# Two bf16 reciprocals moved as one 32-bit word, and the softmax scale carried by the state

## The chip, the cores and the metric

The kernel runs on one core of a Trainium2 chip. Its metric is the device time of one execution in microseconds, as the median of several runs; lower is better. The core has a matrix engine (TensorE; PE in the profile, with PEld for its weight loads), a vector engine (DVE), an activation engine (ACT), a general engine (POOL) and a queue engine (SP) that issues most of the transfers.

## The reference

Two stages: an attention in both directions between the tokens x and a small state, for 8 batches of 8 heads, 512 tokens, 32 state rows and 64 features; then a two-layer network with a leaky rectifier over the result.

```python
scale = 1.0 / np.sqrt(D)                                   # D = 64, so 1/8
scores = scale * np.matmul(x, state.transpose(0, 1, 3, 2))
a = softmax over the 32 state rows (max subtracted, sum + 1e-9)
xread = np.matmul(a, state)
scores2 = scale * np.matmul(state, x.transpose(0, 1, 3, 2))
a2 = softmax over the 512 tokens (the same form)
sread = np.matmul(a2, x)
attn = np.concatenate([xread, sread], axis=2)
x = attn.transpose(0, 2, 1, 3).reshape(B * S, H * D)       # 4352 rows of 512
h = x @ w_in                                               # 512 -> 2048
out = np.maximum(0.01 * h, h) @ w_out                      # 2048 -> 512
```

The two softmax lines are shortened here. Inputs and output are fp32; the products run on bf16 operands.

## The kernel before

**What is multiplied.** The kernel never forms xread. For each batch it forms M = state times w_in, head by head (`a_m`, L376), a matrix of 256 rows (8 heads of 32 state rows, in two groups of 128) by 2048 columns. The first layer is then M transposed times aT, where aT holds the probabilities of the first softmax (`ff1`, L397). ACT applies the leaky rectifier to each product and writes hT in bf16 (L403; L415 for pairs; L967 for the quads of batch 0; L571 for batch 7). The second layer (L608 for batch 0, L679 for the others) uses a form with seven products in place of eight, for which DVE forms sums of parts of hT (`su`, L668) and of w_out (`tw`, L645). The rows of the state (sread) go through the network at the end on their own (`FastIn`, rectifier at L492); that part uses x and w_in alone and not the state tiles.

**The state.** It comes in three pieces. Batches 0 and 1 are loaded first (st0f), cast to bf16 by DVE (stb0, L772) and transposed by PE (`state01`, L160). Batches 2 and 3, and then 4 to 7, are loaded by SP (stf), cast by POOL (stb, L186) and transposed by a DMA that SP issues (st_t, L187). Both the scores (`a_scores`, L216) and M (L376) take their weights from these tiles.

**The first softmax, for batches 1 to 7**, lies over a [128, 1024] tile `sc` of scores: the partitions are 4 groups (two heads each, one of each half of the row) of 32 state rows, the columns are tokens. The maximum over 32 partitions comes from a reduce of DVE that transposes 32x32 blocks (L226); the result has one column for each block of 32 tokens. A broadcast transpose (L234) spreads it again over the 32 rows, DVE subtracts (L239), ACT takes the exponential (L246). The sum goes the same way: a transposing reduce (L251), a small epsilon (L255), a reciprocal in bf16 (L258), a broadcast transpose that spreads it (qb, L263) and the product aT = e1 * qb (L264).

**The second softmax** lies along the columns of the same scores: a maximum with a minus sign (mcol, L288), its scaling (mcols, L290), and the exponential on ACT with this as its bias and the scale as its factor (L296).

**Batch 0** is done apart, at the start, with PE spreading the maxima and reciprocals (L826) and its own exponential (`exp0`, L850).

**The order.** Every engine's instructions run in the order of the source text; nothing is reordered. The loop over batches b = 2 to 7 interleaves, in 16 steps s, the first layer of batch b, the second layer of batch b - 1, and the attention of batch b + 1. The numbers PACE say how many units of the second layer follow each step. `a_probs` stands at s = 7 for most batches, so aT of the next batch is made half a turn before it is used; for batches 1 and 2 it stands ahead of the loop, close before its use. `state_t(0)` (L186 and L187 for batches 2 and 3) is issued between two sums of POOL and its casts of x; `state_t(1)` at b = 2, s = 4.

```python
    weights_sum(1, 0, 4, nc.gpsimd)
    state_t(0)
    ...
    for h in range(NK, H):
        cast_x(2, h, h + 1, POO)
    a_open(a2, 2)
    a_xt_dma(a2)
    ...
    a_probs(a1)
    ...
    pm = a_m(a2, 0, "sc")
    ff(0)
```

At the very start PE runs idle matmuls (`spin`, L142), seven before the transposition of the state and three behind it.

Of the kernel before, what the change touches and what calls it, by code (L numbers as in the profile page):

```python
# [9 lines left out]
P = 128  # L10
B, H, S, D = 8, 8, 512, 64
NS = 32
# [5 lines left out]
SCALE = 1.0 / (D ** 0.5)  # L18
# [4 lines left out]
BF16 = mybir.dt.bfloat16  # L23
FP32 = mybir.dt.float32
AF = mybir.ActivationFunctionType
ALU = mybir.AluOpType
AX = mybir.AxisListType
# [3 lines left out]
def kernel(  # L31
# [9 lines left out]
    nc = tc.nc  # L41
# [4 lines left out]
    att = ctx.enter_context(tc.tile_pool(name="att", bufs=2))  # L46
# [10 lines left out]
    VEC, SCA, POO = nc.vector.tensor_copy, nc.scalar.copy, nc.gpsimd.tensor_copy  # L57
# [4 lines left out]
    st0f = consts.tile([P, 4, D], FP32, name="st0f", tag="st0f")  # L62
# [91 lines left out]
    stb0 = consts.tile([P, 4, D], BF16, name="stb0")  # L154
# [18 lines left out]
    stf = [consts.tile([P, hi - lo, P], FP32, name=f"stf{lo}", tag=f"stf{lo}") for lo, hi in groups]  # L173
    stb = [consts.tile([P, hi - lo, P], BF16, name=f"stb{lo}") for lo, hi in groups]
# [8 lines left out]
                )  # L183

    def state_t(i):
        POO(stb[i][:], stf[i][:])  # L186
        nc.sync.dma_start_transpose(st_t[i][:], stb[i][:].rearrange("p b q -> p (b q)"))  # L187


# [4 lines left out]
    def a_open(a, b):  # L194
        a.b = b
        a.xb = xs[b]
        a.xT = att.tile([P, NT, NK, P], BF16, name="xT", tag="xT")
# [45 lines left out]

    def block_exp(sh, n):
        e1 = att.tile([P, n * NS], BF16, name="e1", tag="e1", bufs=1)
        nc.scalar.activation(out=e1[:], in_=sh[:], func=AF.Exp, scale=SCALE)  # L246
        return e1

    def block_recip(e1, n):
        r1 = att.tile([P, n], FP32, name="r1", tag="r1")  # L250
        nc.vector.tensor_reduce(  # L251
            out=r1[:], in_=e1[:].rearrange("p (c j) -> p c j", j=NS),
            axis=AX.X, op=ALU.add, apply_transpose=True,
        )
        nc.vector.tensor_scalar(out=r1[:], in0=r1[:], scalar1=1e-9, scalar2=None, op0=ALU.add)  # L255
        q1h = att.tile([P, n], BF16, name="qh", tag="qh")
        with nc.allow_low_precision(reason="one rounding, of the finished reciprocal"):
            nc.vector.reciprocal(q1h[:], r1[:])  # L258
        return q1h

    def block_probs(dst, e1, q1h, n):
        q1b = att.tile([P, n, NS], BF16, name="qb", tag="qb", bufs=1)
        nc.vector.transpose(q1b[:], q1h[:, :, None].to_broadcast([P, n, NS]))  # L263
        nc.vector.tensor_tensor(  # L264
            out=dst, in0=e1[:].rearrange("p (g s) -> p g s", g=2),
            in1=q1b[:].rearrange("p (g c) j -> p g (c j)", g=2), op=ALU.mult,
        )

    def a_shift(a, part=None):
# [14 lines left out]
            block_probs(a.aT[:], a.e1, a.q1h, NB)  # L284

    def a_max2(a):
        m2 = att.tile([P, 2], FP32, name="mcol", tag="mcol")
        nc.vector.tensor_reduce(out=m2[:], in_=a.sc[:], axis=AX.X, op=ALU.max, negate=True)  # L288
        a.m2s = att.tile([P, 2], FP32, name="mcols", tag="mcols")
        nc.vector.tensor_scalar(out=a.m2s[:], in0=m2[:], scalar1=SCALE, scalar2=None, op0=ALU.mult)  # L290

    def a_exp2(a, g):
        if g == 0:
            a.e2 = att.tile([P, 2, S], BF16, name="e2", tag="e2", bufs=3)
            a.r2 = att.tile([P, 2], FP32, name="r2", tag="r2", bufs=3)
        nc.scalar.activation(  # L296
            out=a.e2[:, g], in_=a.sc[:, g, :], func=AF.Exp,
            bias=a.m2s[:, g:g + 1], scale=SCALE, accum_out=a.r2[:, g:g + 1],
        )

    def a_probs2(a):
# [92 lines left out]
    def ff1(a, hT, j, later=False):  # L394
        ph = psum.tile([P, S], FP32, name="ph", tag="ph")
        for g in range(2):
            nc.tensor.matmul(  # L397
                ph[:], lhsT=a.M[:, g, P * j:P * (j + 1)],
                rhs=a.aT[:, g, :],
                start=(g == 0), stop=(g == 1),  # L400
            )
        def relu():
            nc.scalar.activation(out=hT[:, j, :], in_=ph[:], func=AF.Prelu, alpha=0.01)  # L403
        return relu if later else relu()

    def ff1_pair(a, hT, j, tag):
        ph = psum.tile([P, 2, S], FP32, name="phw", tag=tag, bufs=1)
        for v in range(2):
            for g in range(2):
                nc.tensor.matmul(  # L410
                    ph[:, v], lhsT=a.M[:, g, P * (j + v):P * (j + v + 1)], rhs=a.aT[:, g, :],
                    start=(g == 0), stop=(g == 1),
                )
        def relu():
            nc.scalar.activation(out=hT[:, j:j + 2, :], in_=ph[:], func=AF.Prelu, alpha=0.01)  # L415
        return relu


    class FastIn:


        R = NK
# [89 lines left out]
    class FastLast:  # L512


        R, Q = 2, S // 2
# [27 lines left out]
        def product(self):  # L543
            r, n = self.todo.pop(0)
            R, Q = self.R, self.Q
            if n == 1:
                self.bank = {
                    k: psum.tile([P, R, Q], FP32, name="pl", tag="ph")[:] for k in (1, 2)
                }
                homes = (("mrowb", 1), ("xT", 2)) if r == 0 else (("e2", 3), ("e2", 3), ("xT", 2))  # L550
                ts = [
                    att.tile([P, (2, 1)[t == "e2"], R * Q], FP32, name="ls", tag=t, bufs=c) for t, c in homes
                ]
                self.sv = dict(zip((1, 6, 5, 7), [t[:, i] for t in ts for i in range(t.shape[1])]))
            bank, sv = self.bank[2 if n in (2, 5, 3) else 1], self.sv
            lhs = {1: self.W[1, 1], 2: self.W[1, 2], 4: self.W[2, 2]}.get(n)
            if lhs is None:
                lhs = self.S[{3: 3, 5: 0, 6: 1, 7: 2}[n]]
            rhs = {1: self.X[1, 1], 2: self.X[2, 1], 3: self.X[2, 2]}.get(n)
            if rhs is None:  # L560
                rhs = self.T[{4: 3, 5: 0, 6: 1, 7: 2}[n]]
            for q in range(R):
                j = R * r + q
                nc.tensor.matmul(  # L564
                    bank[:, q, :], lhsT=lhs[:, P * j:P * (j + 1)], rhs=rhs,
                    start=(n in (1, 2, 5) and q == 0), stop=True, skip_group_check=True,
                )
            flat = bank.rearrange("p q t -> p (q t)")

            def relu(i, c, src):  # L570
                nc.scalar.activation(  # L571
                    out=self.hT[:, 8 * i + R * r:8 * i + R * (r + 1), Q * c:Q * (c + 1)],
                    in_=src.rearrange("p (q t) -> p q t", q=R), func=AF.Prelu, alpha=0.01,
                )

            if n in (1, 6, 7):
                SCA(sv[n], flat)
                self.flush()
            elif n == 5:
                VEC(sv[n], flat)  # L580
            if n in (2, 3):
                k = {2: 1, 3: 6}[n]
                nc.vector.tensor_tensor(out=sv[k], in0=flat, in1=sv[k], op=ALU.add)
                self.late.append((relu, 0, n - 2, sv[k]))
            elif n == 7:
                nc.gpsimd.tensor_tensor(out=sv[5], in0=sv[7], in1=sv[5], op=ALU.add)
            elif n == 4:
                relu(1, 0, flat)
                self.flush()
                self.late.append((relu, 1, 1, sv[5]))  # L590
# [178 lines left out]

    open_xb(0)  # L770
    a_open(a0, 0)
    VEC(stb0[:], st0f[:])  # L772
    spin(7, "py")
    state01()
    spin(3, "py")
# [31 lines left out]
    scn, e10, r0, qb0, m0 = {}, {}, {}, {}, {}  # L807
# [39 lines left out]

    def exp0(u):
        e10[u] = att.tile([P, 2, HT], BF16, name="e0", tag="e0")
        nc.scalar.activation(out=e10[u][:], in_=scn[u][:], func=AF.Exp, scale=SCALE)  # L850

    def eps0(u):
        r0[u] = psum.tile([P, NG], FP32, name="r0", tag="py")
# [73 lines left out]
    q = recip0(0)  # L927
# [7 lines left out]
    q = recip0(1)  # L935
# [6 lines left out]
    class Quad:  # L942
# [21 lines left out]
        def relu(self):  # L964
            n = NK // len(self.tiles)
            for i, t in enumerate(self.tiles):
                nc.scalar.activation(  # L967
                    out=h0[:, self.j + n * i:self.j + n * (i + 1), HT * self.u:HT * (self.u + 1)],
                    in_=t, func=AF.Prelu, alpha=0.01,
                )  # L970

    def m0_evict(c, pm):
# [149 lines left out]
    for b in range(2, B):  # L1122
        hT = hpool.tile([P, 16, S], BF16, name="hT", tag="hT")
        a = att_of[b]
# [14 lines left out]
        for s in range(16):  # L1139
            fast = nxt is None and 4 <= s < 12  # L1140
            if fast:
                n = 1 if s in (7, 11) else 2
# [127 lines left out]
    u, v = [psum.tile([P, 1, HC], FP32, name="yu", tag="ph")[:] for _ in range(2)]  # L1270
# [8 lines left out]
    for n in (1, 2, 6, 5, 7, 3, 4):  # L1279
# [7 lines left out]
        elif n == 7:  # L1287
            nc.gpsimd.tensor_tensor(
                out=ysb[1][:, :, HC:], in0=fs.sv[7][:], in1=fs.sv[5][:], op=ALU.add
# [46 lines left out]
```

## Time and profile before

| what | value |
|---|---|
| runs, median of 3 | 202.02 us (201.66 to 202.12) |
| profiled execution, span from first to last instruction | 199.8 us |
| the profiled execution's own time | its page gives the span alone |
| granted TensorE clock | 1.00 |
| transfers | 28.01 MB, 140 GB/s on average |

A row of the groups is read thus: line, engine, operation, output tile and input tiles, shape of output and input, count, then busy time in us, mean ns of one instruction, and the engine's idle time just ahead of these instructions with what ended it. A row of the timeline has the start in us from the span's start, the length in us, and the instructions merged in it. PE's matmuls overlap in their pipeline, so one matmul of 512 columns is listed with some 380 ns while a row of them advances faster.

### The profile page before, as it was taken

How to read it: one execution, taken by the hardware profiler on the slowest of the kernel's cores; microseconds unless marked ns; L12 is line 12 of the kernel's file. 1: busy time of each engine (PE TensorE's matmuls, PEld its weight loads, DVE VectorE, ACT ScalarE, POOL GpSimd, SP SyncE). 2: the span in 40 equal slices, each digit the busy share in tenths (PEclk: the TensorE clock that was granted, in tenths of full speed). 3: DMA queues.
4: the chain of work that ended last, by engine and by line, in shares of the span. 5: the costliest groups of instructions: out<-in, count | busy, mean ns of one | idle time of the engine just before them, and what ended most of it. 6: DMA issues, size and time to landing. Idle time of an engine off the chain costs nothing.

```text
span 199.8 us, 4974 instructions
## 1 busy us (share of the span) xinstructions
PE 193.2 (97%) x2044; PEld 134.3 (67%) x2066; DVE 160.8 (80%) x249; ACT 143.5 (72%) x263; POOL 55.4 (28%) x82
## 2 busy tenths in 40 slices
PE   7999999999999999999999999999999999999993
PEld 2566633446676767766776677667767788799882
DVE  2676689999999989966997499879978977995622
ACT  3478748599877867877797859787878768767710
POOL 8483174690027004200320041100020024005250
PEclk9999999999999999999999999999999999999999
DMA  5999997999581993269414945290025102210035
GB/s 195 221 206 271 236 296 137 221 286 202 112 223 28 302 266 73 47 213 272 91 24 195 241 43 107 105 164 0 0 108 157 30 0 94 119 56 0 0 95 171
DMA packets 39510, 28.01 MB, mean 140 GB/s; under 512 B 25344, under 2 KB 36736, under 8 KB 39488
## 3 DMA queue, kind: packets, MB, share of 16 engines
q1 hardware_dynamic: 33712, 20.35, 40.8%
q0 software_dynamic: 4944, 6.55, 16.0%
q10 hardware_dynamic: 832, 0.79, 1.2%
q8 instruction: 16, 0.26, 0.5%
q14 instruction: 6, 0.05, 0.1%
HBM read 17.30 MB, written 8.91 MB: 131 GB/s over the span
## 4 chain that ended last, share of the span: by engine, by line
PE 96%; DVE 1%; issue 1%; ACT 1%
PE yq L679 44%; PE ph L397 20%; PE pm L376 4%; PE py L608 4%; PE pyw L608 4%; PE pf L475 3%; PE yu L679 3%; PE ph L958 3%; PE pspin L142 2%; PE pl L564 2%; PE sc L216 1%; PE psn L342 1%; PE php L958 1%; PE phw L410 1%; PE scn L826 1%
## 5 line engine op out<-in xcount | busy, mean ns | idle before, releaser
L403 ACT ACTIVATE hT<-ph 128x512 bf16<-128x512 f32 x100 | 58.5, 605 | 18.4 <-PE ph L397 11.9
L679 PEld LDWEIGHTS <-su 128*128 128x128 bf16 x480 | 45.9, 98 | 14.8 <-DVE su L668 0.8
L397 PE MATMUL ph<-aT,M 128*128 128x512 bf16 x180 | 54.4, 379 | 0.3
L679 PEld LDWEIGHTS <-hT 128*128 128x128 bf16 x336 | 32.3, 98 | 14.3 <-issue 2.5
L679 PE MATMUL yq<-tw_xf,su 128*128 128x256 bf16 x224 | 31.6, 273 | 0.3
L679 PE MATMUL yq<-w_out_bf,hT 128*128 128x256 bf16 x224 | 31.0, 273 | 0.1
L113 POOL CAST xb<-xl 128x512 bf16<-128x512 f32 (+1 forms) x24 | 13.9, 621 | 49.9 <-DMA xl<-in_x_dram 36.7
L668 DVE TENSOR_TENSOR su<-hT 128x1024 bf16<-128x1024 bf16 (+1 forms) x27 | 19.3, 718 | 6.7 <-ACT hT L403 6.7
L397 PEld LDWEIGHTS <-M 128*128 128x128 bf16 x200 | 19.5, 98 | 5.7 <-DVE aT L264 0.2
L751 POOL TENSOR_TENSOR yo<-sv,sv 128x512 f32<-128x512 f32 x7 | 9.1, 1295 | 39.2 <-ACT sv L688 19.4
L688 ACT COPY sv<-yq 128x512 f32<-128x512 f32 x28 | 16.3, 586 | 3.0 <-PE yq L679 2.5
L679 PE MATMUL yq<-w_out_bf,su 128*128 128x256 bf16 x112 | 15.3, 273 | 0.3
L679 PE MATMUL yq<-tw_x,su 128*128 128x256 bf16 x112 | 15.5, 273 | 0.0
L691 DVE TENSOR_TENSOR yo<-yq,sv 128x512 f32<-128x512 f32 x20 | 13.6, 681 | 1.5 <-PE yq L679 1.5
L679 PE MATMUL yq<-tw_x,hT 128*128 128x256 bf16 x104 | 14.5, 273 | 0.0
L390 ACT CAST M<-pm 128x1024 bf16<-128x1024 f32 x12 | 12.2, 1018 | 0.2 <-PE pm L376 0.2
L296 ACT ACTIVATE e<-sc,mcols 128x512 bf16<-128x512 f32 x16 | 11.0, 695 | 0.6 <-DVE mcols L290 0.6
L608 PEld LDWEIGHTS <-hT 128*128 128x128 bf16 x64 | 5.9, 98 | 7.0 <-issue 1.1
L668 DVE TENSOR_TENSOR su<-su,hT 128x1024 bf16<-128x1024 bf16 x14 | 9.7, 692 | 0.5
L288 DVE TENSOR_REDUCE mcol<-sc 128x2 f32<-128x1024 f32 x8 | 9.7, 1214 | 0.0
L226 DVE TRANSPOSE_TENSOR_REDUCE mrow<-sc 128x32 f32<-128x1024 f32 x7 | 8.7, 1240 | 0.5 <-PE sc L216 0.5
L668 DVE TENSOR_TENSOR su<-hT,su 128x2048 bf16<-128x2048 bf16 (+1 forms) x8 | 9.1, 1132 | 0.0
(173 smaller groups left out, 302.6 us busy)
## 6 DMA issues: line engine op xcount, KB each, us to landing
out_dram<-yo SPq DMA_DIRECT2D x12, 512.0 KB, 2.7
xl<-in_x_dram SPq DMA_DIRECT2D x5, 1024.0 KB, 6.7
w_in_bf<-in_moe_w_in_dram POOLq DMA_DIRECT2D x4, 512.0 KB, 7.8
w_out_bf<-in_moe_w_out_dram POOLq DMA_DIRECT2D x2, 512.0 KB, 12.9
x<-in_x_dram POOLq DMA_DIRECT2D x2, 512.0 KB, 11.5
w_out_bf<-in_moe_w_out_dram POOLq DMA_DIRECT2D x4, 256.0 KB, 13.7
xl<-in_x_dram POOLq DMA_DIRECT2D x1, 1024.0 KB, 16.4
out_dram<-ysb SPq DMA_DIRECT2D x4, 256.0 KB, 5.6
```

Source lines behind the costliest of these rows:

```text
L113: copy(xs[b][:, :, h0:h1].rearrange("p t h d -> p h t d"), xl[b][:, h0:h1].rearrange("p h (t d) -> p h t d", t=NT),)
L288: nc.vector.tensor_reduce(out=m2[:], in_=a.sc[:], axis=AX.X, op=ALU.max, negate=True)
L296: nc.scalar.activation(out=a.e2[:, g], in_=a.sc[:, g, :], func=AF.Exp, bias=a.m2s[:, g:g + 1], scale=SCALE, accum_out=a.r2[:, g:g + 1],)
L390: copy(a.M[:, :, cols], pm[:])
L397: nc.tensor.matmul(ph[:], lhsT=a.M[:, g, P * j:P * (j + 1)], rhs=a.aT[:, g, :], start=(g == 0), stop=(g == 1),)
L403: nc.scalar.activation(out=hT[:, j, :], in_=ph[:], func=AF.Prelu, alpha=0.01)
L608: nc.tensor.matmul(y.py, lhsT=hT[:, j, P * i:P * (i + 1)], rhs=w_out_bf[:, j, :], start=(j == 0), stop=(j == 15),)
L668: (eng or nc.vector).tensor_tensor(out=S[n][:, ms], in0=u[:, ms], in1=v[:, ms], op=op)
L679: nc.tensor.matmul(bank[:, i, :], lhsT=lhs[:, m, P * i:P * (i + 1)], rhs=rhs[:, m, :], start=(first and m == 0 and (i == 0 or of is not No ...
L688: copy(t[:], bank)
L691: nc.vector.tensor_tensor(out=dst, in0=bank, in1=self.sv[n][:], op=ALU.add)
L751: nc.gpsimd.tensor_tensor(out=self.yo(1)[:, :, HC:], in0=f.sv[7][:], in1=f.sv[5][:], op=ALU.add)
```

## The change

There are two parts.

The scale 1/8 is put into the bf16 state tiles as they are made: the two casts (L186 on POOL, L772 on DVE) become multiplications by the constant. The scores come out scaled, so the exponentials (L246, L296, L850) lose their factor, and the scaling of the column maxima (L290) is dropped. M comes out scaled as well, so the rectifiers of the token rows (L403, L415, L571, L967) take a factor of 8 ahead of the rectifier. The factor is a power of two.

The reciprocals of the first softmax are spread two at a time. The transposing reduce (L251) now views the columns as blocks of 64 tokens and steps over them by twos, so that the sums of the tokens 2j and 2j + 1 lie side by side. Their bf16 reciprocals form one 32-bit word, and the broadcast transpose (L263) moves 512 such words for each partition rather than 1024 bf16 values. The product (L264) reads the result again as bf16.

```diff
 state_t
-        POO(stb[i][:], stf[i][:])
+        nc.gpsimd.tensor_scalar(out=stb[i][:], in0=stf[i][:], scalar1=SCALE, scalar2=None, op0=ALU.mult)
 block_exp
-        nc.scalar.activation(out=e1[:], in_=sh[:], func=AF.Exp, scale=SCALE)
+        nc.scalar.activation(out=e1[:], in_=sh[:], func=AF.Exp)
 block_recip
-            out=r1[:], in_=e1[:].rearrange("p (c j) -> p c j", j=NS),
+            out=r1[:], in_=e1[:].rearrange("p (c j i) -> p c i j", j=NS, i=2),
 block_probs
-        q1b = att.tile([P, n, NS], BF16, name="qb", tag="qb", bufs=1)
-        nc.vector.transpose(q1b[:], q1h[:, :, None].to_broadcast([P, n, NS]))
+        q1b = att.tile([P, n // 2, NS], FP32, name="qb", tag="qb", bufs=1)
+        pairs = q1h[:].bitcast(FP32)
+        nc.vector.transpose(q1b[:], pairs[:, :, None].to_broadcast([P, n // 2, NS]))
...
-            in1=q1b[:].rearrange("p (g c) j -> p g (c j)", g=2), op=ALU.mult,
+            in1=q1b[:].rearrange("p c j -> p (c j)").bitcast(BF16).rearrange("p (g s) -> p g s", g=2), op=ALU.mult,
 a_max2
-        m2 = att.tile([P, 2], FP32, name="mcol", tag="mcol")
-        nc.vector.tensor_reduce(out=m2[:], in_=a.sc[:], axis=AX.X, op=ALU.max, negate=True)
-        a.m2s = att.tile([P, 2], FP32, name="mcols", tag="mcols")
-        nc.vector.tensor_scalar(out=a.m2s[:], in0=m2[:], scalar1=SCALE, scalar2=None, op0=ALU.mult)
+        a.m2 = att.tile([P, 2], FP32, name="mcol", tag="mcol")
+        nc.vector.tensor_reduce(out=a.m2[:], in_=a.sc[:], axis=AX.X, op=ALU.max, negate=True)
 a_exp2
-            bias=a.m2s[:, g:g + 1], scale=SCALE, accum_out=a.r2[:, g:g + 1],
+            bias=a.m2[:, g:g + 1], accum_out=a.r2[:, g:g + 1],
 ff1 (and in the same way ff1_pair, FastLast and Quad)
-            nc.scalar.activation(out=hT[:, j, :], in_=ph[:], func=AF.Prelu, alpha=0.01)
+            nc.scalar.activation(out=hT[:, j, :], in_=ph[:], func=AF.Prelu, scale=1.0 / SCALE, alpha=0.01)
 the start
-    VEC(stb0[:], st0f[:])
+    nc.vector.tensor_scalar(out=stb0[:], in0=st0f[:], scalar1=SCALE, scalar2=None, op0=ALU.mult)
 exp0
-        nc.scalar.activation(out=e10[u][:], in_=scn[u][:], func=AF.Exp, scale=SCALE)
+        nc.scalar.activation(out=e10[u][:], in_=scn[u][:], func=AF.Exp)
```

More of the change, by code (lines that the diff above doesn't have):

```diff
@@ L414, in relu @@
         def relu():
-            nc.scalar.activation(out=hT[:, j:j + 2, :], in_=ph[:], func=AF.Prelu, alpha=0.01)
+            nc.scalar.activation(out=hT[:, j:j + 2, :], in_=ph[:], func=AF.Prelu, scale=1.0 / SCALE, alpha=0.01)
         return relu
@@ L572, in relu @@
                     out=self.hT[:, 8 * i + R * r:8 * i + R * (r + 1), Q * c:Q * (c + 1)],
-                    in_=src.rearrange("p (q t) -> p q t", q=R), func=AF.Prelu, alpha=0.01,
+                    in_=src.rearrange("p (q t) -> p q t", q=R), func=AF.Prelu, scale=1.0 / SCALE, alpha=0.01,
                 )
@@ L968, in relu @@
                     out=h0[:, self.j + n * i:self.j + n * (i + 1), HT * self.u:HT * (self.u + 1)],
-                    in_=t, func=AF.Prelu, alpha=0.01,
+                    in_=t, func=AF.Prelu, scale=1.0 / SCALE, alpha=0.01,
                 )
```

## The prediction

> **What bounds the kernel now.** I read the page's busy shares and the chain that ended last first, then the busy time by stretches, then what the weight loads of TensorE (PEld) waited for (us in total, times, longest), and only then the single rows of the operations that are edited.
>
> ```profile
> PE 193.2 (97%) x2044; PEld 134.3 (67%) x2066; DVE 160.8 (80%) x249; ACT 143.5 (72%) x263; POOL 55.4 (28%) x82
> ...
> PE 96%; DVE 1%; issue 1%; ACT 1%
> ```
>
> The chain runs through PE for 96% of the span of 199.8 us. DVE, from which nearly everything is taken here, is busy 80% of the time and holds 1% of the chain. An average can hide a stage in which DVE ends last, so the stretches come next.
>
> ```profile
> core 0: us, PE busy (x) PEld busy (x) DVE busy (x) ACT busy (x) POOL busy (x), PEclk, DMA share, GB/s
> ...
> 10.00:17.00 7.00, 6.69 (x137) 4.53 (x130) 5.04 (x11) 5.62 (x11) 5.15 (x7) 1.00 1.24 206
> 17.00:36.00 19.00, 18.84 (x157) 9.43 (x160) 15.22 (x22) 12.68 (x25) 7.43 (x9) 1.00 1.05 237
> 36.00:60.00 24.00, 23.74 (x210) 14.25 (x213) 23.59 (x31) 20.18 (x35) 10.02 (x10) 1.00 0.89 208
> 60.00:100.00 40.00, 39.69 (x415) 27.97 (x420) 35.41 (x53) 30.98 (x57) 9.40 (x13) 1.00 0.63 162
> 100.00:140.00 40.00, 39.68 (x414) 27.81 (x418) 33.39 (x47) 31.59 (x59) 5.28 (x6) 1.00 0.49 109
> 140.00:160.00 20.00, 19.84 (x231) 14.11 (x233) 17.96 (x34) 15.95 (x30) 1.26 (x1) 1.00 0.25 74
> 160.00:185.00 25.00, 24.95 (x286) 22.10 (x286) 20.25 (x30) 18.44 (x35) 6.32 (x5) 1.00 0.14 54
> ```
>
> Between 17 and 185 us PE is idle for 0.16 + 0.26 + 0.31 + 0.32 + 0.16 + 0.05 = 1.26 us in all, at a granted clock of 1.00. That is the ceiling on what any relief of another engine can bring there. Note 36 to 60 us: DVE is busy for 23.59 of 24.00 us and PE still for 23.74. DVE is full there, but just keeps up. What it keeps up with is seen in the waits of the weight loads:
>
> ```profile
> PEld L216 <- DMA xT<-xb: 0.8, 2, 0.4
> PEld L160 <- DVE stb L772: 0.8, 1, 0.8
> PEld L679 <- DVE su L668: 0.8, 2, 0.4
> ```
>
> A load runs beside the previous matmul, so a wait of a load is a bound on a wait of PE, not the wait itself. DVE's sums (su) come in just as they are wanted, twice; the cast of the state (stb) ends a wait once, at the start.
>
> **The change part by part.** First the DVE edits in the attention of batches 1 to 7, by the groups of instructions kept apart by shape (busy us, mean ns of one, idle time before).
>
> ```profile
> L234 DVE STREAM_TRANSPOSE mrowb<-mrow 128x1024 f32<-128x1024 f32 x7 | 8.7, 1245 | 0.2
> L263 DVE STREAM_TRANSPOSE qb<-qh 128x1024 bf16<-128x1024 bf16 x7 | 8.7, 1243 | 0.2
> ...
> L251 DVE TRANSPOSE_TENSOR_REDUCE r<-e 128x32 f32<-128x1024 bf16 x7 | 8.6, 1234 | 0.0
> L239 DVE TENSOR_TENSOR sh<-sc,mrowb 128x1024 f32<-128x1024 f32 x7 | 8.6, 1223 | 0.2
> ...
> L691 DVE TENSOR_TENSOR yo<-yq,sv 128x512 f32<-128x512 f32 x20 | 13.6, 681 | 1.5 <-PE yq L679 1.5
> ...
> L290 DVE TENSOR_SCALAR mcols<-mcol 128x2 f32<-128x2 f32 x8 | 2.0, 245 | 0.3
> ```
>
> The spreading transpose (L263) goes from 1024 16-bit elements to 512 32-bit ones. L234 does the same broadcast transpose on 1024 fp32 elements in 1245 ns against 1243 ns for bf16, so the price goes by elements, not by bytes. For the slope I take the two fp32 rows of one operation: (1223 - 681) / 512 = 1.06 ns per element. A transpose of 512 is then 1243 - 542 = about 700 ns, an estimate, and seven of them free 7 x 0.54 = 3.8 us of DVE. The bounds are 622 ns (half) and 1243 ns (no gain). The multiply behind it (L264) reads the same bytes in the same order and stays.
>
> The reduce (L251) now steps over every second bf16: 1024 elements as before, 4 bytes apart. No row shows a bf16 operand read with a gap. L234 and L239 read fp32 words 4 bytes apart at 1.2 ns per element, and L251 reads dense bf16 at the same 1.2, so packing buys it nothing now and I take 0 for the stride. The bounds are 0 and another 1.23 us each (every element paid twice). [...]
>
> The scaling of the column maxima (L290) goes: 8 x 245 ns = 2.0 us of DVE. Together DVE falls from 160.8 to about 155.0 us. Little of this can reach PE. It is hidden wherever PE runs without a gap, and that is everywhere but the 1.26 us above; were DVE the bound in batches 1 and 2, it would be worth 2 x (0.54 + 0.25) = 1.6 us. The nearest place is the first attention, of batch 1, in the timeline (start us, length us):
>
> ```profile
> 30.00 1.06 ACT L246 ACTIVATE e<-sh 128x1024 bf16<-128x1024 f32 x1 [0.37 <-DVE sh L239]
> ...
> 30.91 1.26 SPq L187 DMA_TRANSPOSE st_t<-stb  x1
> ...
> 31.13 0.17 DVE L290 TENSOR_SCALAR mcols<-mcol 128x2 f32<-128x2 f32 x1
> 31.21 1.24 DVE L251 TRANSPOSE_TENSOR_REDUCE r<-e 128x32 f32<-128x1024 bf16 x1
> ...
> 31.89 1.44 POOL L113 CAST xb<-xl 128x256 bf16<-128x256 f32 x4 [1.00 <-DMA xl<-in_x_dram]
> ...
> 34.37 0.69 DVE L264 TENSOR_TENSOR aT<-e,qb 128x1024 bf16<-128x1024 bf16 x1
> ...
> 35.02 0.11 PEld L376 LDWEIGHTS <-st_t 64*32 64x32 bf16 x8 [0.42 <-DMA st_t<-stb]
> ...
> 35.36 0.55 PEld L397 LDWEIGHTS <-M 128*128 128x128 bf16 x4 [0.23 <-DVE aT L264]
> ```
>
> The probabilities aT are done at 34.37 + 0.69 = 35.06 and the first weight load that waits for them starts at 35.36, behind PE's own product at 35.02. After the change aT comes at about 35.06 - 0.54 - 0.08 = 34.4 (dropping L290 moves the reduce by 0.08 only, from 31.21 to 31.13, since the exponential ends at 31.06). What is late next is PE itself, still in its matmuls. Gain 0 to 0.2 us; I take 0.
>
> Next the scale on ACT. The exponentials lose a constant scale, 124 rectifiers (L403, L415, L571, L967) gain one.
>
> ```profile
> L403 ACT ACTIVATE hT<-ph 128x512 bf16<-128x512 f32 x100 | 58.5, 605 | 18.4 <-PE ph L397 11.9
> ...
> L850 ACT ACTIVATE e<-scn 128x512 bf16<-128x512 f32 x2 | 1.2, 597 | 1.9 <-PE scn L826 1.9
> ```
>
> L850 is an activation of a PSUM tile of this size with a constant scale, L403 one without: 597 and 605 ns. The scale costs nothing that these rows show, and ACT idles 18.4 us ahead of L403 alone. Price 0, within 124 x 8 ns = 1 us either way on an engine with 56 us free.
>
> The start: the state of batches 0 and 1 is now multiplied on DVE (L772) rather than cast.
>
> ```profile
> L772 DVE CAST stb<-st0f 128x256 bf16<-128x256 f32 x1 | 0.5, 546 | 2.4 <-DMA st0f<-in_state_dram 2.4
> ...
> L120 DVE CAST xb<-xf 128x256 bf16<-128x256 f32 x5 | 1.2, 298 | 0.8 <-DMA xf<-in_x_dram 0.8
> ```
>
> And its surroundings in the timeline:
>
> ```profile
> 1.20 3.17 PE L142 MATMUL pspin<-idle 128*128 128x512 bf16 x7 [1.20 <-DVE warm L76]
> ...
> 4.30 0.34 PEld L160 LDWEIGHTS <-stb 128*64 128x64 bf16 x8 [0.84 <-DVE stb L772]
> ```
>
> This one is on PE's path: the load at 4.30 starts when stb is there, and the seventh idle matmul ends at 1.20 + 3.17 = 4.37 by the model, so there is neither cover nor much to gain. The same shape takes 298 ns at L120 and took 546 here. A multiply at one element per 1.06 ns is 681 - 256 x 1.06 = 410 ns, or 658 ns with the 248 ns that L772 took above L120. So -0.1 to +0.1 us; I take 0, since the multiply meets the same neighbours as the cast.
>
> Last, POOL's cast of the later states (L186) becomes a multiply. POOL has no row of a multiply by a constant.
>
> ```profile
> L751 POOL TENSOR_TENSOR yo<-sv,sv 128x512 f32<-128x512 f32 x7 | 9.1, 1295 | 39.2 <-ACT sv L688 19.4 <-issue 18.9 <-POOL ls L586 0.9
> ...
> L186 POOL CAST stb<-stf 128x512 bf16<-128x512 f32 x1 | 1.1, 1067 | 0.0
> ...
> L186 POOL CAST stb<-stf 128x256 bf16<-128x256 f32 x1 | 0.4, 396 | 0.0
> ```
>
> The first, for batches 2 and 3, ends at 30.9, and SP issues its transpose at 30.91. Behind it on POOL stand the casts of x for batch 2, which wait another 1.00 us for their load anyway. The transpose lands here:
>
> ```profile
> st_t<-stb SPq DMA_TRANSPOSE x1, 3.7
> ```
>
> So st_t is there at 34.6 and PE loads it at 35.02: 0.4 us of cover, and from a POOL time of 0.40 + 0.42 = about 0.8 us on, PE waits. Bounds: 0.40 us (the cast) to 1.30 us (a two-input sum of twice the elements), which is 0 to +0.5 us. I take 0.5 us for the multiply, near the cast, as one input is read, and 0 for the time. The second one feeds scores just ahead of this piece of the chain:
>
> ```profile
> L187 SPq DMA_TRANSPOSE st_t<-stb x2: 1189/1226/1262, 30.9 to 62.4; - x2
> ...
> 72.08 0.63 PE psn L342 x64
> ```
>
> Its transpose is issued at 62.4, some 9 us ahead; even a doubled 1.07 us is covered. [...]
>
> Sum against the profiled span: 199.8 + 0 (DVE) + 0 (ACT) + 0 (start) + 0 (POOL) = 199.8 us. The median of the runs is 202.02 us, 2.2 us above the span, which I take as what lies around it. Forecast 202.0 us.
>
> **The rivals.** *A, DVE was binding after all: faster.* For it: DVE full from 36 to 60 us, sums just in time. Against it: 1.26 us of PE idle time over six stretches, much of it with no DVE wait beside it. The loads' waits for su are 0.8 us and for aT 0.2; removing all gives 202.0 - 1.0 = 201.0 us.
>
> *B, the strided reduce is slow: slower.* One mechanism: L251 at twice its time. In batch 1, aT comes at 35.06 + 1.23 - 0.54 - 0.08 = 35.67, its load at 35.97 instead of 35.36: +0.6 us. Batch 2 adds 1.23 - 0.54 - 0.17 = 0.5 us to a DVE that is full, ahead of sums that were just in time. 202.0 + 1.1 = 203.1 us. It decides once a reduce costs over 0.6 us more than now; the later batches have time to spare.
>
> *C, POOL's multiply holds PE up: slower.* From 0.8 us on, at the upper bound +0.5: 202.5 us. For it: POOL's two-input sum takes 1295 ns; against it: its one-input cast takes 396.
>
> *D, it doesn't do what it says:* the 32-bit transpose stays at 1243 ns. Then DVE loses only 2.0 us and the time is 202.0 as well; it goes with the forecast.
>
> **How the numbers follow.** About 0.2%, 0.4 us, is what a measurement of this kernel can tell from no change. Forecast with D: 0.53. A: 0.17, all of it faster. B: 0.14 and C: 0.16, both slower, of C 0.03 for much longer POOL times. The likeliest case alone spans 201.6 to 202.4. The range takes in nearly all of C, B up to its price, and the near end of A: 201.3 to 203.1. So faster 0.17, same 0.53, slower 0.30.
>
> **What would show it.** Right: L263 at about 0.7 us, L251 still at 1.23, no L290, DVE near 155 us, ACT's rectifiers at 605 ns, PE busy time and its idle 1.26 us in the middle unchanged, POOL's scaled cast under 0.8 us. Wrong: L251 above 1.85 us with weight loads of L397 or L679 waiting for aT or su; a load of L376 near 35 us waiting for st_t by more than 0.42; PE's idle time between 17 and 60 us well under 0.42 us together with a shorter span; or pst starting more than 0.1 us away from 4.30.

## The result, and the profile after

| kernel | median of the runs | lowest to highest | ratio to before, with its 95% interval |
|---|---|---|---|
| before | 201.72 us (21 runs) | 201.56 to 202.12 | 1 |
| changed | 202.03 us (21 runs) | 201.62 to 202.43 | 1.0014 [1.0007, 1.0020] |

The change costs 0.28 us (0.0014 x 201.72). That is inside the 0.2% taken for "no change", but the interval lies above 1: with 21 runs of each, the slower side shows. That the median falls on the forecast of 202.0 us is partly luck: the three runs known then had put the kernel before at 202.02 us, 0.3 us above its median over 21.

The page of the changed kernel, the busy times and the chain's shares:

```profile
PE 194.4 (97%) x2066; PEld 134.1 (67%) x2066; DVE 155.1 (78%) x241; ACT 143.5 (72%) x263; POOL 59.3 (30%) x82
...
PE 94%; DMA 2%; DVE 1%; ACT 0%; issue 0%; ACTq 0%
```

DVE went from 160.8 to 155.1 us, and the end did not come sooner. The busy time by stretches of the changed kernel, in the columns shown before:

```profile
17.00:36.00 19.00, 19.00 (x162) 9.42 (x160) 15.09 (x22) 12.86 (x26) 7.92 (x9) 1.00 1.06 238
36.00:60.00 24.00, 24.00 (x214) 14.23 (x213) 22.50 (x30) 20.27 (x36) 10.27 (x10) 1.00 0.87 209
...
17.00:185.00 168.00, 168.00 (x1728) 115.63 (x1726) 140.22 (x205) 129.90 (x239) 43.63 (x43) 1.00 0.57 138
```

PE has no idle time left from 17 to 185 us in this execution, which looks as if 1.26 us had been won. It had not. The count behind the busy time tells why: before had 210 matmul records from 36 to 60 us, this one 214, and over the page 2044 against 2066, the number of weight loads in both. Twenty-two records were missing, 20 of them in the first layer, whose two groups in the kernel before are:

```profile
L397 PE MATMUL ph<-aT,M 128*128 128x512 bf16 x180 | 54.4, 379 | 0.3
...
L397 PEld LDWEIGHTS <-M 128*128 128x128 bf16 x200 | 19.5, 98 | 5.7 <-DVE aT L264 0.2
```

A missing record reads as idle time. A kernel that adds only eight tiny memsets to the one before (before_plus8, below) has its 2066 records and no idle time there; two rows of its view by stretches:

```profile
36.00:60.00 24.00, 24.00 (x214) 14.13 (x213) 23.52 (x31) 19.97 (x35) 9.94 (x9) 1.00 0.95 210
60.00:185.00 125.00, 125.00 (x1355) 91.81 (x1353) 107.16 (x161) 96.62 (x178) 23.19 (x26) 1.00 0.44 109
```

So the ceiling of the prediction on the gain was itself too high: PE had nothing to give back there. The groups of the changed kernel, kept apart by shape:

```profile
L402 ACT ACTIVATE hT<-ph 128x512 bf16<-128x512 f32 x100 | 58.6, 604 | 18.7 <-PE ph L396 18.2
...
L251 DVE TRANSPOSE_TENSOR_REDUCE r<-e 128x32 f32<-128x1024 bf16 x7 | 8.7, 1237 | 0.1
L265 DVE TENSOR_TENSOR aT<-e,qb 128x1024 bf16<-128x1024 bf16 x7 | 5.3, 763 | 0.2
L264 DVE STREAM_TRANSPOSE qb<-qh 128x512 f32<-128x512 f32 x7 | 5.0, 710 | 0.2
...
L186 POOL TENSOR_SCALAR stb<-stf 128x512 bf16<-128x512 f32 x1 | 1.9, 1917 | 0.0
...
L186 POOL TENSOR_SCALAR stb<-stf 128x256 bf16<-128x256 f32 x1 | 0.9, 857 | 0.0
...
L771 DVE TENSOR_SCALAR stb<-st0f 128x256 bf16<-128x256 f32 x1 | 0.3, 294 | 2.8 <-DMA st0f<-in_state_dram 2.8
```

The spreading transpose takes 710 ns, the strided reduce 1237 and the rectifier 604, as forecast. POOL's multiplies take about twice their casts, 857 for 396 and 1917 for 1067 ns. Only the smaller pair is a steady price: over all the profiles below the larger cast took 608 to 1140 ns and the larger multiply 1487 to 1984. The timeline around the first attention (start, length):

```profile
28.28 2.13 POOL L644 TENSOR_TENSOR tw_xf<-w_out_bf,tw_x 128x1024 bf16<-128x1024 bf16 x1
...
30.39 0.86 POOL L186 TENSOR_SCALAR stb<-stf 128x256 bf16<-128x256 f32 x1
...
31.27 1.27 SPq L187 DMA_TRANSPOSE st_t<-stb  x1
...
33.36 2.01 SPq L200 DMA_TRANSPOSE xT<-xb  x1
33.90 0.69 DVE L265 TENSOR_TENSOR aT<-e,qb 128x1024 bf16<-128x1024 bf16 x1
...
35.20 0.11 PEld L375 LDWEIGHTS <-st_t 64*32 64x32 bf16 x8 [0.42 <-DMA st_t<-stb]
...
36.14 2.13 POOL L644 TENSOR_TENSOR tw_x<-tw_xf,w_out_bf 128x1024 bf16<-128x1024 bf16 x1 [2.80 <-DVE tw_xf L644]
...
38.23 0.11 PEld L216 LDWEIGHTS <-st_t 64*32 64x32 bf16 x8 [0.42 <-issue]
```

aT comes 0.47 us sooner (33.90 for 34.37), PE's loads do not. The load for st_t waits the same 0.42 us. What did move is the last row but one: POOL's sum waits for DVE's, and starts at 36.14 rather than 36.55. This profiled execution took 201.72 us, one of the short ones of the changed kernel, and holds nothing that would explain 0.28 us: PE's load of the scores (L216) is 0.17 us later than in the kernel before, but PE was as late already at its load of st_t (35.20 for 35.02), and did not wait for x. The runs that follow had to find it.

### The profile page after: what moved, and what is told of

It is laid out like the page before. It is cut to its first block, busy times and chain, and to the rows that moved or that the text cites. A ratio compares the mean times of both kernels' runs of the same rounds, so it can differ in the third digit from the quotient of the medians.

```text
span 200.0 us, 4988 instructions
## 1 busy us (share of the span) xinstructions
PE 194.4 (97%) x2066; PEld 134.1 (67%) x2066; DVE 155.1 (78%) x241; ACT 143.5 (72%) x263; POOL 59.3 (30%) x82
## 4 chain that ended last, share of the span: by engine, by line
PE 94%; DMA 2%; DVE 1%; ACT 0%; issue 0%; ACTq 0%
PE yq L678 43%; PE ph L396 22%; PE pm L375 4%; PE py L607 4%; PE pyw L607 4%; PE pf L474 3%; PE yu L678 3%; PE ph L957 3%; DMA xf<-in_x_dram 2%; PE pl L563 2%; PE sc L216 1%; PE psn L341 1%; PE php L957 1%; PE phw L409 1%; PE pxth L784 1%; PE scn L825 1%
## 5 line engine op out<-in xcount | busy, mean ns | idle before, releaser
L396 PE MATMUL ph<-aT,M 128*128 128x512 bf16 x200 | 57.7, 379 | 0.0
L113 POOL CAST xb<-xl 128x512 bf16<-128x512 f32 (+1 forms) x24 | 15.0, 668 | 48.3 <-DMA xl<-in_x_dram 48.3
L750 POOL TENSOR_TENSOR yo<-sv,sv 128x512 f32<-128x512 f32 x7 | 10.4, 1493 | 38.0 <-ACT sv L687 18.9
L295 ACT ACTIVATE e<-sc,mcol 128x512 bf16<-128x512 f32 x16 | 11.0, 695 | 0.0
```

Source lines behind the costliest of these rows:

```text
L113: copy(xs[b][:, :, h0:h1].rearrange("p t h d -> p h t d"), xl[b][:, h0:h1].rearrange("p h (t d) -> p h t d", t=NT),)
L295: nc.scalar.activation(out=a.e2[:, g], in_=a.sc[:, g, :], func=AF.Exp, bias=a.m2[:, g:g + 1], accum_out=a.r2[:, g:g + 1],)
L396: nc.tensor.matmul(ph[:], lhsT=a.M[:, g, P * j:P * (j + 1)], rhs=a.aT[:, g, :], start=(g == 0), stop=(g == 1),)
L750: nc.gpsimd.tensor_tensor(out=self.yo(1)[:, :, HC:], in0=f.sv[7][:], in1=f.sv[5][:], op=ALU.add)
```

## The experiments

Ratios are to the kernel before on the same chip in the same rounds.

**Which part.** Four kernels take one part alone: the spread as 32-bit words; all of the scale; only DVE's cast of the first state made a multiply, by 1.0; only POOL's casts made one.

```diff
 pairs_only (to the kernel before): L251, L263, L264 as in the change, nothing else
 scale_only (to the kernel before): all else of the change, L251, L263, L264 as they were
 stb0_by_one
-    VEC(stb0[:], st0f[:])
+    nc.vector.tensor_scalar(out=stb0[:], in0=st0f[:], scalar1=1.0, scalar2=None, op0=ALU.mult)
 pool_by_one
-        POO(stb[i][:], stf[i][:])
+        nc.gpsimd.tensor_scalar(out=stb[i][:], in0=stf[i][:], scalar1=1.0, scalar2=None, op0=ALU.mult)
```

> The kernel before with the 32-bit spread alone (strided reduce, transpose of 512 words); no scale is moved. Start theory (the loss of 0.3 us is made in the first 9 us, by the multiply that replaces the cast of the first state): ratio 1.000, qb transpose 0.71 us, PE's weight loads from 10 us on at the times of the kernel before within run-to-run shifts of the first loads. DVE theory (the strided reduce or the shifted DVE order costs the 0.3 us): ratio 1.0014.

> The changed kernel with the 16-bit spread put back: the scale in the state on DVE and POOL, the factor 8 in the rectifiers. Start theory: ratio about 1.0014, as the whole change. DVE theory: 1.000. POOL theory (the multiply on POOL holds something up): 1.0014.

> The kernel before with one instruction changed: the first state is multiplied by 1.0 on DVE rather than cast. Start theory: ratio about 1.0014, the first PE transposes of x end later. POOL theory and DVE theory: 1.000.

> The kernel before with one instruction changed: POOL multiplies the later states by 1.0 rather than casting them. POOL theory: ratio about 1.0014, with PE waiting for st_t near 35 us. Start theory: 1.000, the POOL multiply at 0.86 and 1.9 us as in the changed kernel, and PE without a new wait near 35 us.

| run | median | ratio |
|---|---|---|
| pairs_only | 201.88 | 1.0006 [0.9997, 1.0015] |
| scale_only | 201.75 | 0.9997 [0.9986, 1.0009] |
| stb0_by_one | 201.76 | 0.9998 [0.9990, 1.0007] |
| pool_by_one | 201.66 | 0.9994 [0.9986, 1.0003] |

No part is slower beyond its interval, so none of these four ratios alone points at a part. The only one above 1 is the spread. POOL's multiply, the suspect of the prediction, is at 0.9994. And the profile of pairs_only has a wait which the kernel before lacks; its timeline:

```profile
33.84 1.87 SPq L200 DMA_TRANSPOSE xT<-xb  x1
...
36.50 2.12 POOL L646 TENSOR_TENSOR tw_x<-tw_xf,w_out_bf 128x1024 bf16<-128x1024 bf16 x1 [2.68 <-DVE tw_xf L646]
...
38.70 0.11 PEld L216 LDWEIGHTS <-st_t 64*32 64x32 bf16 x8 [0.69 <-DMA xT<-xb]
38.70 0.41 PE L216 MATMUL sc<-xT,st_t 64*32 64x512 bf16 x8 [0.20 <-DMA xT<-xb]
```

The scores of batch 2 wait for xT, the transposed x. The same rows of the kernel before (POOL's sum is L645 there):

```profile
36.55 2.13 POOL L645 TENSOR_TENSOR tw_x<-tw_xf,w_out_bf 128x1024 bf16<-128x1024 bf16 x1 [3.22 <-DVE tw_xf L645]
...
38.06 0.11 PEld L216 LDWEIGHTS <-st_t 64*32 64x32 bf16 x8 [0.42 <-DMA xT<-xb]
38.06 0.41 PE L216 MATMUL sc<-xT,st_t 64*32 64x512 bf16 x8
```

**What of the whole must stay for the loss to stay.** after_again is the changed kernel unaltered; the others put back one thing in it. The two with a cast leave out the scale of the batches concerned.

```diff
 after_pool_cast
-        nc.gpsimd.tensor_scalar(out=stb[i][:], in0=stf[i][:], scalar1=SCALE, scalar2=None, op0=ALU.mult)
+        POO(stb[i][:], stf[i][:])
 after_stb0_cast
-    nc.vector.tensor_scalar(out=stb0[:], in0=st0f[:], scalar1=SCALE, scalar2=None, op0=ALU.mult)
+    VEC(stb0[:], st0f[:])
 after_keep_mcols
+        a.m2s = att.tile([P, 2], FP32, name="mcols", tag="mcols")
+        nc.vector.tensor_scalar(out=a.m2s[:], in0=a.m2[:], scalar1=1.0, scalar2=None, op0=ALU.mult)
...
-            bias=a.m2[:, g:g + 1], accum_out=a.r2[:, g:g + 1],
+            bias=a.m2s[:, g:g + 1], accum_out=a.r2[:, g:g + 1],
```

> The changed kernel, unaltered, beside the kernel before on one chip again. If the loss is the change's own, ratio 1.001 to 1.002 again; if it came from that comparison alone, 1.000 within 0.001. Its profile: no wait of PE between 40 and 185 us in either case; the start ends 0.1 to 0.5 us late, and where the run is a long one, PE waits near 38 us for the transposed x of batch 2 (xT), as the kernel with the spread alone did by 0.27 us.

> The changed kernel, but POOL casts the states of batches 2 to 7 and leaves out their scale (those batches are computed without 1/8). If POOL's 0.86 us multiply takes the cover of st_t near 35 us or delays the transposes behind it when DVE runs ahead, the loss goes: ratio 1.000. If not, as the changed kernel, 1.0014.

> The changed kernel, but DVE casts the state of batches 0 and 1 and leaves out their scale. Start theory: the first casts of x end at 6.6 to 6.8 us rather than at 6.9 to 7.0, and the ratio falls from 1.0014 to about 1.0004. POOL theory and the theory of a DVE that runs ahead: 1.0014 stays.

> The changed kernel with the small DVE instruction on the column maxima kept (times 1.0), so that DVE runs ahead by 0.17 us less for each batch and ACT's second exponential waits for it as before. If the loss comes from the order in which ACT and DVE get ahead, it shrinks: ratio near 1.0007. Else 1.0014.

| run | median | ratio |
|---|---|---|
| after_again | 201.90 | 1.0009 [1.0000, 1.0018] |
| after_pool_cast | 201.96 | 1.0007 [0.9998, 1.0016] |
| after_stb0_cast | 201.93 | 1.0008 [0.9999, 1.0017] |
| after_keep_mcols | 201.97 | 1.0010 [1.0001, 1.0019] |

Nothing that is put back brings the time back: with one part less the ratio is 1.0007 to 1.0010, beside 1.0009 for the whole change. So neither multiply nor the dropped scaling of the maxima is seen to carry the loss, though the intervals leave room for a part of it. In three of the four profiles PE waits for xT as in pairs_only: its load waits 0.58 to 0.84 us rather than 0.42. In after_again's it does not, and that execution took 202.03 us all the same. The timeline of after_pool_cast:

```profile
33.64 1.90 SPq L200 DMA_TRANSPOSE xT<-xb  x1
...
36.19 2.12 POOL L644 TENSOR_TENSOR tw_x<-tw_xf,w_out_bf 128x1024 bf16<-128x1024 bf16 x1 [2.58 <-DVE tw_xf L644]
...
38.52 0.11 PEld L216 LDWEIGHTS <-st_t 64*32 64x32 bf16 x8 [0.84 <-DMA xT<-xb]
38.52 0.41 PE L216 MATMUL sc<-xT,st_t 64*32 64x512 bf16 x8 [0.35 <-DMA xT<-xb]
```

The DMA issues give the time from issue to landing, of after_pool_cast:

```profile
xT<-xb SPq DMA_TRANSPOSE x1, 4.8
```

and of the kernel before:

```profile
xT<-xb SPq DMA_TRANSPOSE x1, 4.3
```

What makes the 0.5 us? The transpose of x reports in 16 parts. In the kernel before they come from 37.58 to 37.68 us. In after_pool_cast fifteen come from 38.09 to 38.20 and the last at 38.48, 0.28 us behind. Among the DMA packets there is one more, an instruction fetch of 8 KB, at 37.70 us; before, that fetch comes at 39.08, behind the transpose. The packets by queue from 36.9 to 38.4 us, of the kernel before and then of after_pool_cast:

```profile
q1 hardware_dynamic: 359, 0.22, 84.2%
```

```profile
q1 hardware_dynamic: 511, 0.24, 76.7%
q14 instruction: 1, 0.01, 1.3%
```

**What moves the fetch.** If it went by the count of instructions, a few memsets would move it. The other kernel takes away the wait instead: a piece of the second layer that stood behind the scores now stands ahead of them, so that PE has work while xT lands.

```diff
 after_plus8, before_plus8, before_plus2 (at the start; 8, 8 and 2 times)
+    dummy = consts.tile([P, 2], FP32, name="dummy")
+    for _ in range(8):
+        nc.vector.memset(dummy[:], 0.0)
 after_scores_later
+    piece(0, h0, 0, 3)
     a_scores(a2)
     a_shift(a2)
     a_max2(a2)
-    piece(0, h0, 0, 3)
```

> The changed kernel with eight 2-column memsets added on DVE at the start, where DVE idles. Fetch theory (DVE, running ahead, asks for its next 8 KB of instructions so early that they arrive on one of the DMA engines at the tail of the transpose of x, batch 2, and hold up its last part by 0.28 us, for which PE waits near 38 us): the fetch comes eight instructions earlier, before 35 us, no wait of PE near 38 us beyond 0.42 in the weight load's row, ratio 1.000. Start theory (the loss is in the first 9 us): ratio stays near 1.0010.

> The kernel before with the same eight memsets, as a control. Both theories: ratio 1.000, instruction fetch before 35 us, xT lands 4.3 us after its issue.

> The kernel before with two such memsets, so that DVE reaches the instruction that asks for the fetch 0.6 to 1.4 us earlier, without any other edit. Fetch theory: the fetch falls between 36.5 and 38 us in place of 39, xT lands 4.7 us after its issue rather than 4.3, ratio 1.0008 or more. Start theory: 1.000.

> The changed kernel with four matmuls of the second layer of batch 0 (0.86 us of PE) moved ahead of the scores of batch 2, so that PE wants xT 0.86 us later. Fetch theory: the wait near 38 us is gone whenever the fetch falls, ratio 1.000 or a little under. Start theory: 1.0010. Against both: DVE gets its scores 0.86 us later where it is full, which may cost up to 0.86 us near 52 us.

| run | median | ratio | fetch at | xT landed after |
|---|---|---|---|---|
| after_plus8 | 201.96 | 1.0005 [0.9994, 1.0016] | 37.47 us | 4.8 us |
| before_plus8 | 201.84 | 1.0001 [0.9992, 1.0011] | 40.30 | 4.3 |
| before_plus2 | 201.89 | 1.0003 [0.9994, 1.0013] | 39.29 | 4.3 |
| after_scores_later | 201.76 | 0.9997 [0.9988, 1.0007] | 37.54 | 4.7 |

The memsets did not bring the fetch ahead, neither to before 35 us nor, in before_plus2, to 36.5 to 38: it does not go by DVE's count, and that guess falls. What it does go with is seen when all profiles are laid side by side. In each of those without memsets on POOL, the fetch comes at 37.2 to 37.9 us where POOL's sum into tw_x starts by 36.50 us, and at 39.1 to 41.2 where that sum starts at 36.54 or later. The two nearest to that border, pairs_only and after_again, are 0.04 us apart in the sum and 1.2 us in the fetch, so the sum marks the order of events and is not shown to release the fetch. One kernel without the 32-bit spread, pool_by_one, is on the early side too (sum at 36.39, fetch at 37.25), and its xT landed after 4.3 us. after_scores_later fits a wait of PE as the loss: xT still lands late, PE's load at 39.30 no longer waits for it, and the ratio is 0.9997. It is no clean test, since the same reordering alone costs time (before_scores_later, below).

**Memsets on POOL, and the lead taken back.** Eight tiny memsets on POOL in front of its sums were to move the fetch to before 34 us, if it is POOL's own, and so to take the loss away. And in the changed kernel, DVE is given 0.94 us of idle work just ahead of its sums for tw_x and tw_xf, twice the 0.47 us by which aT had come sooner. If the running ahead is the cause, more work must make it faster. The last kernel does the reordering on the kernel before.

```diff
 after_pool_plus8, before_pool_plus8 (ahead of weights_sum(2, 0, 4, nc.gpsimd))
+    dummy = consts.tile([P, 2], FP32, name="dummy")
+    for _ in range(8):
+        nc.gpsimd.memset(dummy[:], 0.0)
 after_dve_delay
+    delay = att.tile([P, 128], FP32, name="delay", tag="delay", bufs=1)
+    for _ in range(4):
+        nc.vector.memset(delay[:], 1.0)
     for n in (2, 1):
         weights_sum(n, 4, 8)
 before_scores_later: the edit of after_scores_later, to the kernel before
```

> The changed kernel with eight 2-column memsets on POOL ahead of its first sum near 26 us, where POOL idles. The eight memsets on DVE moved nothing (fetch at 37.5, xT 4.8 us), so the fetch is not DVE's by count. POOL theory of the fetch (it is POOL's next 8 KB of instructions, asked for near its sum that starts at 36.1): the fetch moves to before 34 us, the sixteen parts of xT land within 0.15 us of each other, no wait of PE near 38 us, ratio 1.000 to 1.0005. If the fetch is another engine's: it stays at 37 to 38 us, xT 4.7 us, ratio 1.0010.

> Control: the kernel before with the same eight memsets on POOL. POOL theory of the fetch: it moves to before 34 us too, nothing else changes, ratio 1.000. If the eight memsets cost time of their own, it shows here.

> The changed kernel with four memsets of 128 columns (some 0.6 us in all) on DVE just ahead of the two sums that POOL waits for, so that DVE gives back what the 32-bit spread gained there. If running ahead is what brings the fetch onto the tail of xT: POOL's sum starts at 36.5 us or later, the fetch falls at 39 us as before, xT lands in 4.3 us, ratio 1.000 to 1.0005, though DVE has more to do. If the 32-bit spread costs time in another way: 1.0010.

> The kernel before with the four matmuls moved ahead of the scores of batch 2, as in after_scores_later (0.9997). As the kernel before hardly waits there, ratio 1.000; then the changed kernel with this order gains nothing over the kernel before with it, and DVE's 5.7 us are worth nothing on PE's path.

| run | median | ratio | xT landed after |
|---|---|---|---|
| after_pool_plus8 | 202.35 | 1.0031 [1.0019, 1.0042] | 5.2 us |
| before_pool_plus8 | 202.15 | 1.0025 [1.0016, 1.0033] | 5.0 |
| after_dve_delay | 201.66 | 0.9997 [0.9988, 1.0005] | 4.3 |
| before_scores_later | 202.54 | 1.0039 [1.0024, 1.0053] | 4.3 |

The memsets on POOL did not move the fetch ahead. They added one: the fetch that otherwise comes at about 59 us is missing there in both profiles, and in its place the changed kernel has two on the tail of xT, at 37.71 and 38.07 us, and the kernel before has one, at 37.32, beside its usual one at 41.04. So a run that was to take the loss away became a larger dose of it: with more fetches on the tail of xT the time rises, in the kernel before as well. The timeline of after_pool_plus8, where two of the sixteen parts come late, at 38.83 and 39.22 us, the others by 38.54:

```profile
39.26 0.11 PEld L216 LDWEIGHTS <-st_t 64*32 64x32 bf16 x8 [1.27 <-DMA xT<-xb]
39.26 0.41 PE L216 MATMUL sc<-xT,st_t 64*32 64x512 bf16 x8 [0.77 <-DMA xT<-xb]
```

Its PE wait of 0.77 us, in the longest of its six runs, stands against 0.0031 x 201.77 = 0.63 us of time. And with the delay the ratio is 0.9997 [0.9988, 1.0005]. That lies below the interval of the changed kernel as first measured (from 1.0007) and overlaps that of after_again (from 1.0000); the unaltered changed kernel did not run beside it. The timeline of after_dve_delay:

```profile
33.83 0.69 DVE L265 TENSOR_TENSOR aT<-e,qb 128x1024 bf16<-128x1024 bf16 x1
...
34.50 0.94 DVE L1050 MEMSET delay<- 128x128 f32 x4
...
36.90 2.13 POOL L644 TENSOR_TENSOR tw_x<-tw_xf,w_out_bf 128x1024 bf16<-128x1024 bf16 x1 [3.26 <-DVE tw_xf L644]
...
38.17 0.11 PEld L216 LDWEIGHTS <-st_t 64*32 64x32 bf16 x8 [0.42 <-DMA xT<-xb]
```

aT is as early as in the changed kernel, the sums are not: POOL starts at 36.90, the fetch comes at 39.19, xT lands in 4.3 us, and the ratio is 0.9997 though DVE was given 0.94 us more to do.

before_scores_later, expected at 1.000, shows where DVE's time is worth something. The same reordering that left the changed kernel at 0.9997 puts the kernel before at 1.0039. Its chain of waits, in order of time (start, length), and then its timeline:

```profile
39.86 1.26 DVE mrow L226
...
41.15 1.26 DVE mrowb L234
...
42.42 1.23 DVE sh L239
43.65 1.14 DVE mcol L288
...
44.81 0.30 DVE mcols L290
45.12 0.60 DVE ysb L618
...
45.76 0.60 PE yq L679 x4
```

```profile
45.02 0.68 DVE L618 COPY ysb<-py 128x512 f32<-128x512 f32 x1
...
45.76 0.49 PE L679 MATMUL yq<-w_out_bf,hT 128*128 128x256 bf16 x3 [0.24 <-DVE ysb L618]
```

The scores come later there, DVE's column of work ends later, and PE waits for its copy (L618). The edited scaling of the maxima (0.30 us) stands in that column; without it, in after_scores_later, the copy starts at 44.62 rather than 45.02 and PE goes on without a gap. In the order as it is, DVE does not bind. The gap of 0.24 us is only a part of the 0.0039 x 201.77 = 0.79 us; another load waits for DVE's sums (su) near 62 us, and the rest was not followed.

**All profiles side by side.** One interval isolates the wait: from PE's load of st_t for batch 2 (35.20 in the changed kernel) to its load of the scores of batch 2 (38.23). It is 3.04 us in the kernel before, and the same in every kernel in the order of the source whose PE waits no longer for xT. In the seven kernels that have the 32-bit spread in that order, without delay or memsets on POOL, it is 3.04 three times (the changed kernel twice, and after_plus8), then 3.19 (after_stb0_cast), 3.30 (pairs_only), 3.37 (after_keep_mcols) and 3.45 (after_pool_cast): 0.17 us more on average. Their seven ratios average 1.0008, which is 0.17 us as well; with one profile for each kernel this is an estimate. From the load of the scores to the end 161.7 us pass in all kernels in that order, so nothing behind it matters.

The largest other difference is the start. PE's first load of st comes at 11.2 to 11.9 us, on average at 11.59 in the ten kernels that multiply the first state and at 11.61 in the eight that cast it: it varies from execution to execution, and not with the change. The two profiles of the changed kernel differ from that of the kernel before by the start alone; their load of the scores comes 0.17 and 0.45 us later without any longer wait for xT. So the wait is seen in four relatives of the changed kernel, and in no profile of the kernel itself.

No kernel here beats the one before: the best ratios (0.9994, and 0.9997 three times) all have 1 in their interval.

## Why the prediction was right and wrong

**The prices held.** The transpose was put at about 700 ns and took 710; DVE at 155.0 us, measured 155.1, and 156.4 in after_again, where the seven products aT alone took 6.0 rather than 5.3 us (last section); the stride was put at 0 and cost 1237 - 1234 = 3 ns; the factor in the rectifier at 0, and it took 604 for 605 ns. Rival B, the slow reduce, and D, the unshortened transpose, are out. Per element the reduce took 1237 / 1024 = 1.21 ns with its bf16 read 4 bytes apart, and 1234 / 1024 = 1.21 ns with the bf16 dense.

**The start** cost nothing that shows, as forecast: stb0_by_one is at 0.9998, and PE's load stands at 4.29 for 4.30 us. The 294 ns of the multiply against 546 of the cast are no price, though: over all profiles the multiply took 293 to 508 ns and the cast 295 to 546.

**POOL's multiply was mis-sized.** I put it at 0.5 us; it took 0.857, past the 0.8 from which C was to decide, and the larger one took 1.917 us, over the 1.30 that was my upper bound for the smaller. It did not decide: the load for st_t waits the same 0.42 us, at 35.20, and pool_by_one is at 0.9994. The prediction let the landing of st_t follow its issue one for one. It did not: issued 0.36 us later (31.27 for 30.91), it landed 0.18 us later (34.78 for 34.60), and in pool_by_one, issued at 31.51, at 34.74. No run shows the much longer POOL times to which C gave 0.03: in the changed kernel POOL's sum ends at 28.28 + 2.13 = 30.41 us, the first multiply starts as it ends, at 30.39, and over all the profiles the longest multiply took 1.984 us.

**The ceiling of 1.26 us, and with it rival A,** rested on missing records. The columns give the count beside the busy time, and 2044 against 2066 stood in the first line that I quoted.

**The step that failed** is the one after aT: "What is late next is PE itself, still in its matmuls. Gain 0 to 0.2 us." It counted PE as the only thing that meets the earlier DVE. DVE's sums behind aT, POOL's sum behind those, an instruction fetch behind that, and the transposed x, whose last part came 0.28 us behind the others with that fetch on its tail (after_pool_cast), follow, and the last is one that PE takes just in time. The row for it stood in the prediction, "PEld L216 <- DMA xT<-xb: 0.8, 2, 0.4", and was never priced: xT landed at 33.35 + 4.3 = 37.65 and its load began at 38.06, so that there was at most 0.4 us of slack, and a transfer 0.5 us late costs 0.1 to 0.5 us, an estimate; the four profiles that show it have 0.15 to 0.41 us. The measured 0.28 us lies there, on an edit whose bounds I had put at a gain of 0 to 0.2. Whether it is this wait in the executions of the changed kernel itself stays open, as its two profiles show PE late by the start alone.

**What is shown and what is not.** Shown by intervention: with an added fetch on the tail of xT the kernel before is slower, at 1.0025 [1.0016, 1.0033], and the changed kernel stands at 1.0031, above both its ratios without it (1.0014 and 1.0009). In line with it, but with intervals that overlap those of after_again and after_plus8: holding the sums back, or giving PE other work while xT lands, leaves the changed kernel at 0.9997. Every one of the seven kernels with the 32-bit spread in the order of the source and without further memsets on POOL or delay is above 1 (1.0005 to 1.0014), the five without it, in the same order, lie at 0.9994 to 1.0003. Not shown: whose instruction fetch this is, and by what it is released, since only its place next to POOL's sum is known; and its share in each execution. In before_pool_plus8's profile PE is idle for only 0.15 us from 36 to 60 us, and its interval up to the scores is 3.26 us, 0.22 longer, against 0.0025 x 201.77 = 0.50 us of time; the rest of that is not accounted for. xT landed in 4.8 or 4.7 us in five of those seven profiles, but in 4.3 in the two of the changed kernel itself, once with the fetch at 37.21 us and no harm, once with the fetch at 39.11. Whether 1.0014 and the 1.0009 of the repeat differ is open, as their intervals overlap.

## What to carry to other kernels

Relief of an engine off the path isn't priced at zero by the engine alone: follow what runs ahead, down to the transfers, and look for one that the bound engine takes with a few tenths to spare. Before idle time of an engine is taken for a ceiling, compare its count of records with that of a partner, such as matmuls with weight loads. Take back the suspected cause by adding work: a delay that makes a kernel faster says more than another part removed, if the kernel without it runs beside it. And when a loss is as small as the spread of the start, cut each profile at fixed instructions and compare the intervals, as the whole span hides it.

## What the runs showed of the hardware

An instruction fetch of 8 KB is listed among the DMA packets, in a queue of its own (q14), its time given as a share of the same 16 engines as that of the data. It took 0.31 to 1.2 us. In six profiles it came at 37.46 to 37.88 us, on the tail of a DMA transpose, whose last part came 0.25 to 0.28 us behind the other fifteen, so that the whole landed in 4.7 to 4.8 rather than 4.3 us. In before_pool_plus8 the last part was 0.64 us behind and the whole took 5.0 us; with two fetches it was 5.2 us. At 37.21 and 37.25 us (the changed kernel, pool_by_one) a fetch did no harm: the transpose landed in 4.3 us.

POOL's multiply of fp32 by a constant with a bf16 result took 857 or 858 ns for 256 elements per partition, about twice its cast (393 to 411). For 512 it took 1487 to 1984 ns.

The product aT, whose edit leaves its shape alone, took 0.69 us in batches 1 to 3 in all 18 profiles, but up to 1.77 us in later ones, with a mean of 763 ns in the changed kernel and 1270 in pairs_only:

```profile
L265 DVE TENSOR_TENSOR aT<-e,qb 128x1024 bf16<-128x1024 bf16 x7 | 8.9, 1270 | 0.2
```

The traces show beside what it is stretched. Of the 126 products 42 took over 0.72 us, and each of these began while POOL was in a sum of two tiles (yo) and ended 0.55 us after that sum. Where POOL's sum began behind the product's start, the product took 0.69 us. So in these traces its end follows that of the sum of POOL that is under way as it starts; in the timeline of pairs_only, 83.16 + 1.65 is 0.55 us past 82.99 + 1.27:

```profile
82.99 1.27 POOL L752 TENSOR_TENSOR yo<-sv,sv 128x512 f32<-128x512 f32 x1 [5.69 <-issue]
...
83.16 1.65 DVE L265 TENSOR_TENSOR aT<-e,qb 128x1024 bf16<-128x1024 bf16 x1
```

PE did not wait for aT there.
